# A block-sparse attention and channel-mixer kernel: another order of steps and other PSUM banks in its hand-written list

## The chip, the core and the metric

The kernel runs on one core of one Trainium2 chip. The engines named below are PE (TensorE, the matrix engine, with its weight loads shown apart as PEld), DVE (VectorE), ACT (ScalarE), POOL (GpSimd) and SP (SyncE, which here only issues DMAs). Each takes its own queue of instructions in order, and semaphores hold an instruction until what it reads is there and what it overwrites has been read. The metric is the device time of one execution in microseconds (us), as the median of several runs.

## The reference

Two layers, one behind the other: an attention under a block mask, and a mixer with a low-rank part along the sequence and a two-layer network along the channels.

```python
B, H, S, D = 4, 8, 768, 64
scores = q @ k.transpose(0, 1, 3, 2) / sqrt(D)
scores = where(mask, scores, -1e9)        # 32x32 blocks: neighbours, first and last, 3 drawn ones a row
attn = exp(scores - max) ; attn = attn / (sum(attn) + 1e-9)
x = (attn @ v).transpose(0, 2, 1, 3).reshape(B, S, 512)

h = x.transpose(0, 2, 1) @ U @ V          # U 768x32, V 32x768
u = x + h.transpose(0, 2, 1)
out = u + maximum(u @ w_ch1, 0) @ w_ch2   # w_ch1 512x2048, w_ch2 2048x512
```

Inputs and output are float32; the output is 4 x 768 x 512.

## The kernel before

The whole program is unrolled in one function. The 32 heads are taken as 16 pairs i = 0 to 15, four (HP) to a batch; a pair's queries and keys lie side by side in 128 partitions. For a pair the scores come out transposed (keys in partitions), so that exp(scores) can serve as the stationary operand of the product with v, whose extra column of ones gives the sums; masked entries are multiplied by 0 after exp. Per batch, the four pairs' results stand in `xf` (float32, one buffer of 128 x 6 x 512 a batch; the pool has two buffers, so batch 2 takes that of batch 0, and batch 3 that of batch 1) and in `xh` (float16). Then come the low-rank mix over the sequence, a transpose by DMA into `uT`, w1 with ReLU into `hid`, w2 into `xf`, and the stores. The w2 products are done in Winograd's form of Strassen's scheme (seven half-size products and sums of operands), as are the w1 products of the last batch. The attention of the next batch runs between the channel products of the one before.

PE, DVE, ACT and SP run in program order (`manual_schedule`, line 1112), and the program order is the string `PLAN` (lines 436 to 517): a loop (lines 1120 to 1131) takes it word by word. A word of capitals and a digit takes the next step of its kind and gives it the PSUM bank of that digit; a word in lower case runs the follow-up, on DVE or ACT, of an earlier product word of its kind, in the order in which these were queued; a word with dots calls a function with the numbers given. POOL is outside this order.

| word | what it issues | line |
|---|---|---|
| S, B, Q, H (plain) | scores of a pair into PSUM; Q (8 matmuls) does two heads in banks 0 to 5 | 951, 970, 1001 |
| e, p | exp on ACT; multiply by the mask on DVE | 960, 1010; 1016 |
| K, k | a part of the mask made on PE, its copy | 1085 on |
| A, V | products with v (V: all 36 matmuls of one head, into the bank of its digit) | 402 |
| v, y | divide on DVE (a reciprocal, then a product that reads the bank and writes `xf`); copy to `xh` on ACT | 532, 539; 537 |
| M, m, F, x, d | low-rank mix: Ut product, its copy on DVE, Vt product of two halves, add to `xf` on DVE, cast to `xh` on ACT | 638, 643, 653, 618, 622 |
| T.i | DMA transpose of pair i's `xh` into `uT`, on SP | 611 |
| U.b.c.j.bank, P, C | w1 product of batch b (4 matmuls of 384 columns) | 673 |
| a.b.c.j.e | its ReLU, e = 0 on DVE, 1 on ACT | 687, 685 |
| S.b.t.k, H.b.t.p.part, D.b.t.k | w2 in Winograd's form: sums of `hid` on DVE, half a product (4 matmuls of 256), add to `xf` on DVE | 843, 748, 867 |
| Z.b.t.u | store of row 2t+u of batch b (256 KB), on SP | 695 |
| L.i | loads(i+1): transposes of the casted q and k of pair i+2 (`qpl`, `kpl`), then loads of q, k and v of pair i+3 (384 KB each), on SP | 375, 150, 161 |
| q.k.n | a sum of weights for Winograd's form, on DVE | 709 |
| t, g, c, o, r, s | last batch: sums of inputs, w1 products, copies, sums, ReLUs, sums of `hid` | 709, 748, 782, 789 |
| h.t.p.part, e.t.k | last batch: quarter of a w2 product (2 matmuls of 256), its add on DVE; e also issues the store of half a row (128 KB) on SP | 748; 891, 893 |

A bank may be written anew only when the follow-up that reads it is done: so the digits decide, with the order, what a PE word waits for. Two more waits matter for the change. The first divide of pair 8 writes batch 2's `xf` and needs the stores `Z.0.*` to have landed, that of pair 12 writes batch 3's and needs `Z.1.*`. And an instruction of SP that waits (a transpose for its casts, or for the last product that reads the old `qpl`) holds every DMA behind it.

The loop that reads the list:

```python
for word in PLAN.split():
    kind = word[0]
    if "." in word:
        fn, *args = word.split(".")
        calls[fn](*map(int, args))
    elif kind.isupper():
        fn, *args = next(steps[kind])
        fn(*args, *map(int, word[1:]))
    elif kind in "ab":
        results["relu"].popleft()(kind)
    else:
        results[kind].popleft()()
```

Of the kernel before, what the change touches and what calls it, by code (L numbers as in the profile page):

```python
# [23 lines left out]
def kernel(  # L24
# [417 lines left out]
    y p H U7 e p H b C e p H b U7 e p H b U6 e p E1 a g p V7 Q v e e V6 U7 v p U0 a P1 b C p P6 a C E7 Q
    a g U6 e e U7 b P6 b p U0 C a U7 p a Q b X6 Y e e P7 y C P6 b C p U0 b a p V7 L.5 Q v U.0.1.3.6 e
    q.3.0 V7 a.0.1.3.0 e U.0.1.1.1 v U.0.1.11.0 a.0.1.1.1 U.0.1.5.6 q.3.1 a.0.1.11.1 p Q a.0.1.5.1 p
    U.0.1.10.6 e U.0.1.7.7 a.0.1.10.0 e U.0.1.2.6 a.0.1.7.0 S.0.0.1.3 U.0.1.9.7 p a.0.1.2.1 Q a.0.1.9.1
    q.7.1 U.0.1.4.6 e S.0.0.2.0 H.0.0.1.0.7 p H.0.0.1.1 a.0.1.4.1 U.0.1.0.0 p L.6 e U.0.1.14.1 q.4.1 V6
    a.0.1.0.1 p a.0.1.14.1 Q v q.4.0 e V6 D.0.0.0 S.0.0.3 H.0.0.6.0 e v U.0.1.13.2 q.7.0 H.0.0.6.1
    U.0.1.12.6 a.0.1.13.1 D.0.0.2 y p Q a.0.1.12.1 q.5.1 H.0.0.7.0 e H.0.0.7.1 q.5.0 H.0.0.5.0.6 D.0.0.3
    H.0.0.5.1 e S.0.0.4.4 U.0.1.6.1 p H.0.0.4.0 a.0.1.6.1 H.0.0.4.1 D.0.0.4 Q D.0.0.5 p H.0.0.3.0 e L.7
    H.0.0.3.1 p H.0.0.2.0.7 H.0.0.2.1 e p U.0.1.8.2 U.0.1.15.0 D.0.0.1 D.0.0.6 a.0.1.8.1 V7 p a.0.1.15.1  # L450
    S.0.1.1.1 Q S.0.2.1.0 V6 e v S.0.1.2.4 H.0.1.1.0.7 y v H.0.1.1.1 y H.0.1.2.0.0 S.0.2.2.3 y H.0.1.2.1
    e D.0.1.0 M6 D.0.1.1 H.0.2.1.0.1 m H.0.2.1.1 S.0.2.3 F.1.0.2.4 D.0.2.0 F.1.1.3.6 F.1.2.5.0 x.6.0
    H.0.2.6.0 x.6.1 d.6.0 H.0.2.6.1 x.7.0 d.6.1 F.1.3.6.4 D.0.2.2 H.0.1.6.0 T.6 x.5.1 H.0.1.6.1 S.0.1.3
    H.0.2.7.0 H.0.2.7.1 x.4.0 H.0.2.5.0.6 x.5.0 H.0.2.2.0.0 D.0.2.3 d.5.0 H.0.2.2.1 x.4.1 d.5.1
    H.0.2.4.0 D.0.1.2 d.4.0 T.5 x.7.1 H.0.2.4.1 d.7.0 H.0.1.7.0 D.0.2.1 d.4.1 D.0.2.5 H.0.1.7.1 d.7.1
    S.0.2.4.2 T.4 Q D.0.1.3 H.0.2.5.1 e H.0.1.4.0 T.7 D.0.2.4 H.0.1.4.1 H.0.2.3.0 e D.0.1.5 H.0.2.3.1
    Z.0.0.1 p H.0.1.5.0.7 Z.0.2.1 H.0.1.5.1 D.0.2.6 Q Z.0.2.0 D.0.1.4 Z.0.0.0 S.0.1.4.0 U.1.0.0.6 e
    H.0.1.3.0 a.1.0.0.0 H.0.1.3.1 e U.1.0.11.6 D.0.1.6 p U.1.0.10.0 Z.0.1.0 Z.0.1.1 a.1.0.11.1 U.1.0.9.7
    p L.8 a.1.0.10.1 U.1.0.6.6 a.1.0.9.1 p Q a.1.0.6.1 p U.1.0.12.6 e V7 e U.1.0.2.2 v U.1.0.5.0 p
    a.1.0.12.1 U.1.0.1.7 a.1.0.5.1 a.1.0.2.1 U.1.0.3.6 a.1.0.1.0 p Q a.1.0.3.1 V6 p e U.1.0.4.7 v e  # L460
    U.1.1.5.2 a.1.0.4.0 U.1.0.15.6 p a.1.1.5.1 U.1.1.9.7 a.1.0.15.1 p Q a.1.1.9.1 U.1.1.3.7 e L.9
# [701 lines left out]
```

## Time and profile before

| quantity | value |
|---|---|
| time of the runs | 274.29, 274.45, 274.58 us; median 274.45 |
| span of the profiled execution | 271.1 us, 7373 instructions |
| DMA | 37.58 MB, mean 139 GB/s |
| HBM read / written | 27.67 / 6.29 MB |
| exp of the Q words (line 1010) | 72 of 1450 ns, 100.6 us on ACT |
| w1 products (line 673) | 384 matmuls of 326 ns from start to end, 70.2 us |
| mask multiply (line 1016) | 72 of 933 ns, 65.5 us on DVE |
| divide's product (line 539) | 32 of 553 ns, 17.7 us on DVE |
| half-row stores (line 893) | 12 of 128 KB, 1.7 us from issue to landing |

The time of a run is that of the whole execution on the device; the span is that of the profiled execution, from its first to its last instruction; 3.35 us lie between the span and the median. Matmuls overlap: a matmul of 384 columns lasts 326 ns from start to end, and four of them follow each other in 0.65 us. What a word costs PE is this pitch, and the ends of its rows overlap with the next one's start. An instruction that reads a matmul's result begins some 0.2 us behind its end. Rows of the timelines begin with the start in us from the start of the span and the length; "x4" is a number of instructions in one row, and square brackets give the idle time before the row and what ended it.

### The profile page before, as it was taken

The page shows a single profiled execution, that of the slowest core. Times are in us where ns is not written, and L with a number is a line of the kernel's source. Part 1 is how long each engine was busy: PE and PEld are TensorE (multiplying, and loading weights), DVE is VectorE, ACT ScalarE, POOL GpSimd, SP SyncE. Part 2 cuts the span into 40 slices and gives each one's busy share as a digit, 9 for nine tenths or more (in the row PEclk, how much of TensorE's full clock was granted, in tenths as well). Part 3 has the DMA queues.
Part 4 walks back from the last instruction along what each step waited for, and adds up shares of the span by engine and source line. Part 5 has one row for each costly group of instructions (what it writes and reads, how often), then busy time and mean ns, then how long its engine had stood idle before and what let it go on. Part 6 is the DMA issues. An engine that isn't in the chain of part 4 may idle for free.

```text
span 271.1 us, 7373 instructions
## 1 busy us (share of the span) xinstructions
PE 261.9 (97%) x3008; PEld 182.1 (67%) x3008; DVE 235.3 (87%) x475; ACT 202.5 (75%) x264; POOL 84.7 (31%) x164
## 2 busy tenths in 40 slices
PE   7899999999999999999999999999999999999993
PEld 3577776555567778565666877565667788657882
DVE  5699988988999998868688997688998999999992
ACT  3889998897989666788888847788997943889100
POOL 4479104931628643035624660044000000000000
PEclk9999999999999999999999999999999999999998
DMA  5799997999974664872527356670200116300024
GB/s 161 239 305 316 199 210 173 225 131 198 155 222 67 201 204 91 278 217 59 178 45 190 64 212 117 221 208 16 46 0 2 41 41 142 134 0 0 22 78 136
DMA packets 49698, 37.58 MB, mean 139 GB/s; under 512 B 30528, under 2 KB 46816, under 8 KB 49664
## 3 DMA queue, kind: packets, MB, share of 16 engines
q1 hardware_dynamic: 46688, 32.67, 45.9%
q0 software_dynamic: 2688, 4.19, 10.9%
q8 instruction: 23, 0.38, 0.6%
q10 hardware_dynamic: 288, 0.24, 0.3%
q14 instruction: 11, 0.09, 0.1%
HBM read 27.67 MB, written 6.29 MB: 125 GB/s over the span
## 4 chain that ended last, share of the span: by engine, by line
PE 72%; DVE 17%; DMA 4%; ACT 2%; issue 1%; SPq 1%; POOL 0%; DVEq 0%; ACTq 0%
PE ps L748 28%; PE ps L673 20%; PE ps L402 9%; PE ps L1001 8%; DVE est L1016 5%; DMA qld<-in_q_dram 3%; PE ps L951 2%; DVE xf L867 2%; DVE xf L539 2%; DVE sums L843 1%; DVE res L709 1%; DMA vld<-in_v_dram 1%; ACT est L1010 1%; PE ps L970 1%; DVE sums L709 1%
## 5 line engine op out<-in xcount | busy, mean ns | idle before, releaser
L1010 ACT ACTIVATE est<-ps 128x1536 f16<-128x1536 f32 x72 | 100.6, 1450 | 18.9 <-PE ps L1001 18.9
L673 PE MATMUL ps<-uT,w1t 128*128 128x384 f16 x384 | 70.2, 326 | 0.2 <-DVE hid L687 0.2
L1016 DVE TENSOR_TENSOR est<-est,mask 128x1440 f16<-128x1440 f16 x72 | 65.5, 933 | 0.2
L673 PEld LDWEIGHTS <-w1t 128*128 128x128 f16 x384 | 35.6, 98 | 26.9 <-issue 7.0
L402 PEld LDWEIGHTS <-est 128*128 128x128 f16 x1152 | 40.2, 97 | 7.2 <-ACT hid L685 1.3
L402 PE MATMUL ps<-vt,est 128*128 128x65 f16 x1152 | 43.3, 193 | 0.1
L142 POOL CAST stqld<-qld 128x192 f16<-128x192 f32 x40 | 19.9, 540 | 73.2 <-DMA qld<-in_q_dram 36.0
L748 PEld LDWEIGHTS <-hid 128*128 128x128 f16 x360 | 34.3, 98 | 7.0 <-issue 1.9
L685 ACT ACTIVATE hid<-ps 128x384 f16<-128x384 f32 x63 | 29.7, 495 | 4.7 <-PE ps L673 4.3
L1001 PE MATMUL ps<-qpl,kpl 64*128 64x512 f16 (+1 forms) x288 | 31.6, 325 | 0.0
L748 PE MATMUL ps<-w2t,hid 128*128 128x256 f16 x240 | 31.3, 273 | 0.2 <-DVE xf L539 0.2
L867 DVE TENSOR_TENSOR xf<-xf,ps 128x256 f32<-128x256 f32 x63 | 25.0, 411 | 3.7 <-PE ps L748 3.3
L687 DVE TENSOR_SCALAR hid<-ps 128x384 f16<-128x384 f32 x33 | 18.2, 553 | 8.1 <-PE ps L673 7.5
L748 PEld LDWEIGHTS <-sums 128*128 128x128 f16 x216 | 20.3, 98 | 4.7 <-issue 1.1
L142 POOL CAST stkld<-kld 128x192 f16<-128x192 f32 x40 | 22.3, 597 | 2.5 <-DMA kld<-in_k_dram 2.5
L960 ACT ACTIVATE est<-ps 128x768 f16<-128x768 f32 x30 | 22.5, 813 | 0.6 <-PE ps L951 0.6
L1001 PEld LDWEIGHTS <-kpl 64*128 64x128 f16 x288 | 12.1, 94 | 14.3 <-issue 9.1
L748 PE MATMUL ps<-res,sums 128*128 128x256 f16 x144 | 19.4, 273 | 0.3 <-DVE xf L867 0.3
L622 ACT CAST xh<-xf 128x384 f16<-128x384 f32 x24 | 11.0, 510 | 10.4 <-DVE xf L618 10.4
L539 DVE TENSOR_TENSOR xf<-ps,rcp 128x384 f32<-128x384 f32 x32 | 17.7, 553 | 0.8
L142 POOL CAST vt<-vld 128x192 f16<-128x192 f32 x40 | 17.9, 487 | 0.0
L748 PE MATMUL ps<-res,hid 128*128 128x256 f16 x120 | 15.9, 273 | 0.0
(121 smaller groups left out, 341.5 us busy)
## 6 DMA issues: line engine op xcount, KB each, us to landing
vld<-in_v_dram SPq DMA_DIRECT2D x16, 384.0 KB, 4.6
qld<-in_q_dram SPq DMA_DIRECT2D x15, 384.0 KB, 3.5
kld<-in_k_dram SPq DMA_DIRECT2D x15, 384.0 KB, 5.5
out_dram<-xf SPq DMA_DIRECT2D x18, 256.0 KB, 2.2
w1t<-in_moe_w_ch_dram POOLq DMA_DIRECT2D x4, 512.0 KB, 8.2
w2t<-in_moe_w_ch_dram POOLq DMA_DIRECT2D x4, 512.0 KB, 10.4
out_dram<-xf SPq DMA_DIRECT2D x12, 128.0 KB, 1.7
qld<-in_q_dram SPq DMA_DIRECT2D x2, 192.0 KB
```

The costliest lines, as they stand in the source:

```text
L142: last = nc.gpsimd.tensor_copy(out=dst[:, h, ts], in_=ld[:, h, ts])
L402: nc.tensor.matmul(pav[:, sc, :], est[:, n, sc * P : (sc + 1) * P], vts[b % 2][:, 2 * hp + h, g, 0 : D + 1], start=(g == 0 and sc == 0), s ...
L539: nc.vector.tensor_tensor(out=dst, in0=pav[:, :, 0:D], in1=rcp[:, :, None].broadcast_to([P, T, D]), op=ALU.mult,)
L673: nc.tensor.matmul(pt, w1t[:, cc, jj * P : (jj + 1) * P], bts[b].uT[:, cc, c * HS : (c + 1) * HS], start=(cc == 0), stop=(cc == NCC - 1), ...
L685: nc.scalar.activation(out=dst, in_=pt, func=AF.Relu)
L687: nc.vector.tensor_scalar_max(out=dst, in0=pt, scalar1=0.0)
L748: nc.tensor.matmul(acc[key], lhsT, rhs, start=(first and i == 0), stop=(i == len(pairs_) - 1), skip_group_check=True,)
L867: nc.vector.tensor_add(out=x, in0=x, in1=acc[a, b, tau])
L960: lambda: nc.scalar.activation(out=dst, in_=ps, func=AF.Exp, scale=0.125),
L1001: nc.tensor.matmul(units[h][:, u * S + lo : u * S + hi], kT[drows[h], g * P : (g + 1) * P], qT[drows[h], lo:hi], start=True, stop=True, sk ...
L1010: nc.scalar.activation(out=both[h], in_=units[h].rearrange("p (g n) -> p g n", g=2), func=AF.Exp, scale=0.125,)
L1016: lambda: nc.vector.tensor_mul(out=masked(both[h]), in0=masked(both[h]), in1=masked(mask[:, 2 * j : 2 * j + 2, :]),),
```

## The change

The diff replaces the string `PLAN`; nothing else in the file differs. The new string is three lines shorter, so that what stands behind it moves up by three lines. It has the same words in another order: as many of each kind, dotted words with the same numbers but for the banks, the same split of ReLUs between DVE and ACT. 130 of the 574 product words name another bank. Most words move a few places. Of SP's DMAs, the stores change their place most: in batch 1 the old list has `Z.1.1.1 T.10 T.8 T.11 T.9 Z.1.1.0 Z.1.0.1 Z.1.2.0 Z.1.0.0 Z.1.2.1 L.12`, the new one `Z.1.1.1 Z.1.0.0 T.8 Z.1.0.1 T.10 T.11 T.9 Z.1.2.0 L.12 Z.1.1.0 Z.1.2.1`. The two products with v of pair 12 (`V6` and `V7` in the old list, with `v` behind each) are both `V7` in the new one. The start, the end of batch 1 with the beginning of pair 12, and the tail:

```diff
--- before.py
+++ after.py
@@ -434,86 +434,83 @@
 
 
     PLAN = """
-    S0 S3 e e S5 B0 e Z7 e S3 z Z6 e z B0 A7 A e R6 S3 t A R5 e A B0 t A K6 e A S3 k v A5 A e K6 k B0 A
-    A e K7 A K6 k S3 k A K7 e v B0 k S3 e M6 e A5 A m R7 A t B0 K6 R3 e k A A t S6 A e v S0 D2 S3 e d A7
-    A e A S0 K6 A e S3 k K2 A e S5 k A e v S3 R2 e S5 t S0 e M7 e S3 m D2 e B5 d A0 D1 e A A d A S3 D2 A
...
-    H.1.0.3.0 D.1.1.4 M4 S.1.2.2.0 H.1.0.3.1 m D.1.1.5 F.2.0.5.4 F.2.1.0.1 D.1.0.6 Z.1.1.1 H.1.2.1.0.6
-    x.8.0 H.1.2.1.1 x.10.0 d.8.0 H.1.1.3.0 x.10.1 d.10.0 F.2.2.7.5 D.1.2.0 F.2.3.4.2 d.10.1 H.1.2.2.0.1
-    x.8.1 T.10 H.1.2.2.1 x.11.0 H.1.1.3.1 x.9.0 d.11.0 H.1.2.6.0 x.11.1 d.8.1 H.1.2.6.1 d.9.0 D.1.1.6
-    T.8 H.1.1.2.0.7 D.1.2.1 d.11.1 x.9.1 H.1.1.2.1 S.1.2.3 d.9.1 Q T.11 D.1.2.2 D.1.1.1 e H.1.2.7.0
-    H.1.2.7.1 T.9 H.1.2.5.0.7 D.1.2.3 e H.1.2.5.1 S.1.2.4.2 H.1.2.4.0 Z.1.1.0 H.1.2.4.1 Z.1.0.1 Q
-    D.1.2.5 D.1.2.4 U.2.0.4.6 p e H.1.2.3.0 a.2.0.4.0 H.1.2.3.1 e U.2.0.12.6 D.1.2.6 U.2.0.5.7 Z.1.2.0
-    Z.1.0.0 a.2.0.12.1 Q Z.1.2.1 a.2.0.5.0 p U.2.0.2.7 e L.12 U.2.1.8.6 a.2.0.2.0 U.2.1.1.7 a.2.1.8.1 e
-    U.2.0.11.2 a.2.1.1.0 U.2.0.15.6 p a.2.0.11.1 U.2.0.0.7 p Q a.2.0.0.1 p a.2.0.15.1 U.2.0.9.7 e V6
-    a.2.0.9.0 p e U.2.0.8.0 v U.2.0.10.7 a.2.0.8.1 U.2.1.4.6 a.2.0.10.0 p Q a.2.1.4.1 V7 p e U.2.1.0.6 v
-    e U.2.0.13.1 a.2.1.0.0 U.2.0.1.7 p a.2.0.13.1 U.2.1.2.6 a.2.0.1.1 p Q a.2.1.2.0 U.2.1.9.7 e L.13
...
-    h.0.3.0 e.1.3 h.0.3.1 h.0.3.2 e.1.4 h.0.3.3 e.0.5 h.2.3.0 h.1.4.0 e.0.6 h.1.4.1 h.1.3.0 h.1.3.1
-    h.1.3.2 h.1.3.3 h.2.4.1 h.2.4.2 h.2.4.3 h.1.4.2 h.1.4.3 e.2.5 h.2.3.1 e.1.6 h.2.3.2 h.2.3.3 e.1.5
-    e.2.6
+    S0 e Z7 z S3 S5 e e B1 e Z0 A7 A A S5 z B0 e e S3 e A R6 t R5 t B0 e K4 k K6 A A v A5 A A k S3 B0 e e K7
+    K3 K4 k k A A A v S6 e B0 M3 m k R7 A5 A A S3 e e B0 e t K7 K3 k k A R4 t S6 A A v S0 e e S2 e D7 d A6 A
+    A S0 S4 K2 k e e A A A v S0 S3 e e R2 t M7 m S5 e S0 S3 e e D2 B5 A0 D1 d d D2 d A A A e S3 A A K1 k S5
...
+    H.1.1.4.0 S.1.2.2.0 y y y M2 m D.1.1.5 Z.1.1.1 H.1.0.3.1 H.1.0.3.0 D.1.0.6 Z.1.0.0 F.2.0.5.0 x.8.0 d.8.0
+    F.2.1.3.2 x.8.1 d.8.1 x.10.1 T.8 x.10.0 d.10.0 d.10.1 Z.1.0.1 T.10 H.1.2.1.0.6 H.1.2.1.1 D.1.2.0
+    H.1.1.3.1 H.1.1.3.0 D.1.1.6 F.2.2.2.7 x.11.0 d.11.0 x.9.0 d.9.0 F.2.3.1.3 x.11.1 d.11.1 T.11 x.9.1 d.9.1
+    T.9 H.1.2.2.0.5 H.1.2.2.1 D.1.2.1 H.1.1.2.0.7 H.1.2.6.0 H.1.2.6.1 D.1.2.2 Q e e S.1.2.3 H.1.1.2.1
+    D.1.1.1 H.1.2.7.0 H.1.2.7.1 D.1.2.3 S.1.2.4.2 H.1.2.5.0.7 H.1.2.5.1 D.1.2.4 H.1.2.4.1 H.1.2.4.0 D.1.2.5
+    p Q e e U.2.0.4.6 a.2.0.4.0 H.1.2.3.0 H.1.2.3.1 D.1.2.6 Z.1.2.0 U.2.0.12.6 a.2.0.12.1 U.2.0.5.7
+    a.2.0.5.0 q.0.1 Q e L.12 Z.1.1.0 U.2.0.2.7 a.2.0.2.0 U.2.1.8.6 a.2.1.8.1 U.2.1.1.7 p a.2.1.1.0 p p p e
+    U.2.0.15.2 a.2.0.15.1 U.2.0.11.1 a.2.0.11.1 U.2.0.0.6 a.2.0.0.1 Q e e U.2.0.9.6 a.2.0.9.0 V7 U.2.1.4.1
+    a.2.1.4.1 U.2.0.8.6 a.2.0.8.1 Q e e p p Z.1.2.1 v U.2.0.10.6 a.2.0.10.0 V7 v y y U.2.1.0.6 a.2.1.0.0
+    U.2.0.13.2 a.2.0.13.1 U.2.0.1.7 a.2.0.1.1 Q e e p p q.0.0 U.2.1.2.7 a.2.1.2.0 U.2.0.7.6 a.2.0.7.0 q.1.1
+    U.2.1.9.7 a.2.1.9.0 p U.2.0.6.0 a.2.0.6.1 U.2.0.14.6 a.2.0.14.1 Q e e p V7 p V6 v y v p U.2.0.3.7
...
+    h.1.2.2 e.1.1 h.2.4.2 h.0.4.3 h.2.3.1 h.0.4.0 h.0.3.0 h.0.4.2 h.0.4.1 h.2.4.3 h.2.3.2 e.0.5 h.0.3.1
+    h.0.3.3 h.0.3.2 e.0.6 e.2.5 h.1.3.0 h.1.3.3 h.1.4.2 h.1.3.2 h.1.3.1 e.1.6 h.2.3.3 h.2.3.0 e.2.6 h.1.4.3
+    h.1.4.0 h.1.4.1 e.1.5
     """
 
     class Pair:
```

More of the change, by code (lines that the diff above doesn't have):

```diff
@@ L442 @@
[L442 to L461, printed above, removed]
@@ new lines @@
+    S.0.0.3 D.0.0.2 H.0.0.7.0 q.7.1 H.0.0.7.1 p p q.5.0 H.0.0.5.0.6 H.0.0.5.1 D.0.0.3 D.0.0.4 p e p
+    U.0.1.6.2 a.0.1.6.1 H.0.0.4.1 Q L.6 L.7 H.0.0.4.0 D.0.0.5 H.0.0.3.0 H.0.0.3.1 D.0.0.6 e p e p
+    H.0.0.2.0.7 H.0.0.2.1 D.0.0.1 U.0.1.8.2 a.0.1.8.1 U.0.1.15.6 a.0.1.15.1 S.0.2.1.0 S.0.1.1.1 S.0.2.2.3 Q
+    e e V7 v y V6 v y H.0.2.1.0.1 H.0.2.1.1 D.0.2.0 S.0.1.2.4 H.0.1.1.0.7 H.0.1.1.1 D.0.1.0 M0 m H.0.1.2.0.3
+    H.0.1.2.1 S.0.2.3 F.1.1.4.2 x.4.1 F.1.0.0.6 x.4.0 d.4.0 d.4.1 x.6.1 d.6.1 T.4 H.0.2.6.1 H.0.2.6.0
@@ new lines @@
+    D.0.2.2 H.0.1.6.1 x.6.0 d.6.0 T.6 F.1.2.5.4 F.1.3.2.0 x.7.1 x.5.1 x.7.0 x.5.0 d.5.0 d.5.1 d.7.0 T.5
+    Z.0.0.0 d.7.1 T.7 Z.0.0.1 H.0.2.7.0 H.0.1.6.0 H.0.2.7.1 D.0.2.3 D.0.1.2 S.0.1.3 H.0.2.5.0.6 H.0.2.2.0.2
+    H.0.2.2.1 D.0.2.1 D.0.1.1 H.0.2.4.1 H.0.2.4.0 D.0.2.5 S.0.2.4.2 H.0.1.7.0 H.0.1.7.1 D.0.1.3 Q e e
+    H.0.2.5.1 D.0.2.4 S.0.1.4.0 H.0.1.4.0 H.0.1.4.1 D.0.1.5 H.0.2.3.0 H.0.2.3.1 D.0.2.6 p H.0.1.5.0.7
+    H.0.1.5.1 D.0.1.4 Q e e U.1.0.0.6 a.1.0.0.0 H.0.1.3.0 H.0.1.3.1 D.0.1.6 Z.0.1.0 U.1.0.6.6 a.1.0.6.1
@@ new lines @@
+    U.1.0.9.1 a.1.0.9.1 U.1.0.11.2 a.1.0.11.1 U.1.0.10.6 a.1.0.10.1 Q e e p p p p p Z.0.2.1 Z.0.2.0 V7
+    Z.0.1.1 v y U.1.0.12.6 a.1.0.12.1 U.1.0.1.2 p a.1.0.1.0 U.1.0.2.0 a.1.0.2.1 U.1.0.5.4 a.1.0.5.1
+    U.1.0.3.7 a.1.0.3.1 Q e V7 v U.1.0.4.6 a.1.0.4.0 p e U.1.0.15.1 a.1.0.15.1 y U.1.1.5.7 a.1.1.5.1
+    U.1.1.9.6 a.1.1.9.1 Q e e U.1.0.7.6 p a.1.0.7.0 U.1.1.3.7 a.1.1.3.0 p p U.1.0.14.6 a.1.0.14.1 U.1.1.4.2
+    a.1.1.4.0 U.1.1.10.1 a.1.1.10.1 U.1.1.1.6 a.1.1.1.1 L.8 Q e e V7 p V6 v U.1.1.7.7 a.1.1.7.1 y Q e e v
@@ new lines @@
+    c.5.1.2 c.3.1.3 c.2.1.1 c.1.1.0 g.0.1.2 c.0.1.9 D.2.2.4 H.2.2.3.1 H.2.2.3.0 Z.2.0.0 t.1 t.2 q.6.1
+    D.2.2.6 g.2.6 g.1.2.7 o.1.1 g.5.2.1 o.5.1 t.4 t.3 c.2.2.4 g.1.6 c.1.2.2 g.5.6 c.5.2.0 g.0.6 g.3.6
+    c.3.2.5 c.0.2.10 g.3.2.4 o.3.1 g.0.2.7 g.1.7 c.1.3.7 g.2.7 o.0.1 c.2.3.9 q.2.1 q.2.0 g.3.7 g.1.5.4 o.1.3
+    r.1.0.0 g.3.5.7 c.3.3.3 o.3.3 r.3.0.0 g.2.4 o.2.4 g.3.4 o.3.4 g.1.4 o.1.4 g.0.7 g.1.3 o.1.2 r.1.1.1
+    g.4.1.6 c.4.1.11 c.0.3.3 g.3.3 o.3.2 r.3.1.0 g.2.5.0 o.2.3 g.5.7 c.5.3.6 g.5.5.4 s.3.1.22 s.3.3 g.6.1.1
```

84 lines of the change are left out of this document (40 added, 44 removed).

## The prediction

> **What bounds the kernel now.** I read the busy times first, then the chain of waits, then the stretches, and last the timelines of the places that the new list touches.
>
> ```profile
> PE 261.9 (97%) x3008; PEld 182.1 (67%) x3008; DVE 235.3 (87%) x475; ACT 202.5 (75%) x264; POOL 84.7 (31%) x164
> PE 72%; DVE 17%; DMA 4%; ACT 2%; issue 1%; SPq 1%; POOL 0%; DVEq 0%; ACTq 0%
> ...
> 0.00:43.00 43.00, 39.39 (x518) 27.72 (x518) 34.65 (x79) 36.83 (x44) 20.55 (x36) 1.00 0.92 238
> 70.00:100.00 30.00, 29.30 (x374) 20.24 (x372) 29.72 (x52) 23.84 (x30) 18.83 (x32) 1.00 0.62 153
> 100.00:224.00 124.00, 123.52 (x1482) 85.51 (x1479) 106.16 (x194) 98.43 (x125) 33.60 (x72) 1.00 0.43 115
> 224.00:267.00 43.00, 42.90 (x342) 32.79 (x336) 39.98 (x108) 21.01 (x46) 0.00 (x0) 1.00 0.23 68
> 267.00:271.00 4.00, 0.00 (x0) 0.00 (x0) 0.36 (x1) 0.00 (x0) 0.00 (x0) 0.84 0.40 133
> ```
>
> The first line is busy time by engine, the second the chain that ended last, the others are stretches (length, then busy us of PE, weight loads, DVE, ACT and POOL, granted clock, DMA share, GB/s). TensorE works in 97% of the span and is 72% of the chain; from 100 to 267 us it lacks 0.6 us of 167. It is short of work only in the first 43 us (3.6 us), between 70 and 100 us (0.7 us, while VectorE is busy 29.72 of 30) and in the last 4 us, which are the final add and its store. The clock is 1.00 until the matmuls end. So a new order gains only in these holes, and loses wherever it lets something come after TensorE needs it.
>
> **What the change does not touch.** Both lists have 1277 words, each kind as often as before: 574 words that issue 3008 matmuls, the same 475 VectorE and 264 ScalarE instructions, 128 DMAs on SP, also the same split of ReLUs between ScalarE and VectorE. TensorE's work is therefore the same to the instruction; GpSimd's queue keeps its order. What is added and removed costs nothing; what moves is priced below, against the 271.1 us of this span. The remaining 3.35 us of the 274.45 median lie around it and stay.
>
> **Part 1: two stores go behind the loads (+1.2).** Pair 12's first divide writes xf of batch 3, whose buffer was batch 1's (two buffers), so it waits until every store of batch 1 has landed. The old list issues all six before L.12; the new one issues Z.1.1.0 after L.12 and Z.1.2.1 later still, both in SP's queue behind two front transposes and three 384 KB loads. SP, loads, VectorE and TensorE there:
>
> ```profile
> 172.43 1.31 SPq L695 DMA_DIRECT2D out_dram<-xf  x3
> 174.12 1.25 SPq L375 DMA_TRANSPOSE qpl<-stqld  x1
> 175.47 1.23 SPq L375 DMA_TRANSPOSE kpl<-stkld  x1
> 176.75 0.58 SPq L150 DMA_DIRECT2D qld<-in_q_dram  x1
> 177.38 0.46 SPq L150 DMA_DIRECT2D kld<-in_k_dram  x1
> 177.88 0.47 SPq L161 DMA_DIRECT2D vld<-in_v_dram  x1
> ...
> 178.00:180.00 2.00, 2.00 (x30) 1.18 (x29) 1.55 (x3) 1.78 (x3) 0.00 (x0) 1.00 0.96 296
> 180.00:182.00 2.00, 2.00 (x36) 1.48 (x32) 1.77 (x4) 2.00 (x3) 1.69 (x4) 1.00 0.81 283
> 182.00:184.00 2.00, 2.00 (x32) 1.11 (x31) 1.87 (x3) 1.06 (x3) 2.00 (x5) 1.00 0.06 19
> ...
> 181.03 0.19 DVE L532 RECIPROCAL rcp<-ps 128x6 f32<-128x6 f32 x1
> 181.25 0.56 DVE L539 TENSOR_TENSOR xf<-ps,rcp 128x384 f32<-128x384 f32 x1
> ...
> 183.43 1.26 PE L402 MATMUL ps<-vt,est 128*128 128x65 f16 x36
> ...
> out_dram<-xf SPq DMA_DIRECT2D x18, 256.0 KB, 2.2
> ```
>
> SP issues one DMA in about 0.45 us here, so the two stores leave at about 178.4 and 178.85, right behind the load of v. The three loads (3 x 393 KB = 1.18 MB) move in 178 to 182: 2 us at 296 GB/s and 2 us at 283 are 1.16 MB, after which the DMA engines idle (0.06). If the stores' packets stand behind the loads' packets, their 2 x 262 KB = 0.524 MB take 1.7 us (at 315 GB/s, the highest slice of the page's first part) to 1.85 us (at 283) from 182 on: landed at about 184.0. The divide (reciprocal to end 0.78) then runs its product from 184.0 to 184.6. The new list puts both value products of pair 12 into bank 7 (before: 6 and 7), so the second one, which stands at 183.43, cannot begin before that divide has read the bank: 184.6 + 0.05 - 183.43 = **1.2 us** of TensorE's time. Waiting with the divide on VectorE are the second head's divide, the mask multiplies of the quads behind it and the ReLUs on VectorE, all of whose readers on TensorE stand behind the second value product and so move with it (the mask multiplies, 0.90 each, serve value products some 4 us later); I count nothing more.
> Bounds: if stores pass the loads, they land 178.85 + 2.2 = 181.05 and nothing waits (0). If each store takes its whole 2.2 us one after the other, after the last load has landed at 177.88 + 4.6 = 182.5, they end at 186.9 and TensorE waits 186.9 + 0.6 + 0.05 - 183.43 = 4.1 us. I take 1.2: the DMA share 0.96 and 0.81 says that the loads fill the engines, the nearest row to what the stores meet.
> [...] The trace's whole store takes 2.2 us, about 0.9 of it data at these rates, so at most 1.3 us is fixed; the sum above has none of it, since the first store's fixed part runs beside the loads.
>
> **Part 2: what the low-rank mix waits for (-0.4).** In batch 2 the old list runs M4, one H word, the copy m (queued behind a pair sum), then F:
>
> ```profile
> 159.07 0.52 PE L638 MATMUL ps<-xh,Ut 128*32 128x128 f16 x24
> 159.17 0.79 DVE L709 TENSOR_TENSOR sums<-sums,hid 128x1024 f16<-128x1024 f16 x1
> ...
> 159.88 0.41 DVE L643 CAST a<-ps 128x256 f16<-128x256 f32 x1
> ...
> 160.34 0.51 PE L653 MATMUL ps<-a,Vt 64*128 64x128 f16 x12 [0.21 <-DVE a L643]
> ```
>
> The H word between (4 matmuls, 0.44 by pitch) ends at 159.95 and F begins 160.34: a hole of 0.39. The new list has M2 with both H words behind it and the pair sum ahead of it. The copy can then start 0.2 after M2's end; M (0.44 by pitch), two H words (0.88) against copy 0.20 + 0.41 + 0.05 = 0.66: F waits for nothing, or 0.1 if the copy stands behind a divide. I take 0.3 of 0.39. In batch 3 the old list has the copy late by 0.24 behind one H word (product at 220.21); with two it is hidden, I take 0.1. Bounds: 0 to -0.63.
>
> **Part 3: the tail (-0.3).** Old: the last two row stores are issued back to back and the very last waits for SP; new: three words h (h.1.4.3, h.1.4.0, h.1.4.1) stand between e.2.6 and e.1.5, which now ends alone.
>
> ```profile
> 265.85 1.51 DVE L891 TENSOR_TENSOR xf<-xf,ps 128x256 f32<-128x256 f32 x4 [1.69 <-PE ps L748]
> 256.00 12.09 SPq L893 DMA_DIRECT2D out_dram<-xf  x12
> ```
>
> The last add ends at 267.36; its store is issued 267.69 to 268.09, because SP was with the one before until 267.60. The three words (2 matmuls each, 0.22 by pitch) put the earlier store 0.66 before the last, longer than SP's 0.40 for it: the 0.33 of waiting goes. Bounds: 0 to -0.33.
>
> **Part 4: the other local moves (+0.2).** From the rows: ScalarE and VectorE start 0.2 us after the end of what they read, TensorE 0.05 after theirs. Walking both new queues along TensorE's old times, product by product, the new order is late at few places after 100 us: a ReLU that stands behind a weight sum by 0.07, a value product that waits for its mask multiply at about 217.6 by 0.12. I take 0.15 of these. In the first 43 us exp and mask copies are late by 0.1 to 0.6 at six places (largest a mask step behind an exp near 14 us), but the old order has waits there too (3.6 us of hole), which the new one meets differently; I take +0.1, bounds -0.6 and +0.6. From 70 to 100 us VectorE is full in both and does the same work: 0, bounds -0.6 (TensorE's hole) and +1.0 (rival C). The transposes T keep their place against their readers (first product that needs one stands 0.2 us behind its landing at about 228.8); stores of batch 2 go later, and nobody waits for that buffer.
>
> **Sum:** 1.2 - 0.4 - 0.3 + 0.15 + 0.1 = about +0.75; 274.45 + 0.75 = **275.2 us**. Its own range: the stall between 0.6 and 2.2 with the rest fixed gives 274.6 to 276.2; 0.6 is half of the stores' bytes getting out beside the loads, 2.2 adds 1.0 of the 1.3 us that a store's 2.2 leave beside its data.
>
> **Rivals.**
> *B, the stores are not held (chance 0.27).* The packets of the stores go out beside those of the loads that were issued before them. For it: vld lands 4.6 us after issue, so three loads were in flight at once in the trace; against it: the engines were at 0.96. Then Part 1 is 0 and the sum -0.45: 274.0. This is the case on the other side; it decides where the stores land before 182.8, so that the divide frees bank 7 by 183.43. Half of it falls under -0.55, half is no change. [...]
> *C, VectorE loses its fill at 70 to 100 us (0.15).* Its slack is 0.28 us there. The same multiplies (0.90), sums (0.68 to 0.79) and divides stand in another order, and one product that waits for a multiply placed behind one more sum of 0.7 costs TensorE this much, not caught up while VectorE is full. On top of A that is 275.2 + 0.8 = 276.0.
> *D, the new order fills the holes (0.08).* Half of the 3.6 + 0.7 us that TensorE lacks before 100 us comes back, about 2 us, with Part 1 small: about 272.5. Against it: the start waits for exp and loads (ScalarE 36.83 of 43, DMA 0.92), whose amount is the same.
> *That the list is only shuffled without effect* is part of "same": 3008 matmuls in the same clock.
>
> **Chances and range.** A 0.50, B 0.27, C 0.15, D 0.08. About 0.2% (0.55 us) is what a measurement can tell from no change: the bounds are 273.9 and 275.0. Faster: D 0.08, half of B 0.13, A's lower end 0.02: 0.23. Same: the other half of B, and of A what falls under 275.0 (0.08): 0.22. Slower: 0.40 of A and C: 0.55. The range reaches from B's lower part, 273.2, to 277.2, where C ends with the long stall (274.45 - 0.45 + 2.2 + 1.0).
>
> **What would show it.** Right: the divide of pair 12's first head starts some 1.2 us after the value products that feed it could let it, after an idle stretch of VectorE ended by a DMA (the store of row 5, Z.1.2.1), and TensorE idles about 1.2 us before the second value product of 36 matmuls; SP's timeline has two stores behind the load of v. F of batch 2 without a wait; the last store issued within 0.1 us of its add. Wrong: no hole near 183 us (B); TensorE busy less than 28.6 of the 30 us from 70 to 100 (C); more than 41 of the first 43 (D).

## The result, and the profile after

The new list is slower. Against the old one on the same chip the ratio of the times is 1.0102, with an interval of 1.0058 to 1.0147 (6 executions each: median 277.7 us against 274.5). Measured again in the last group of experiments, with 12 executions, the ratio was 1.0048 (1.0017 to 1.0079; 276.7 against 274.9). Both intervals hold 1.006 to 1.008, some 1.6 to 2.2 us. (A ratio is not the quotient of the two medians beside it, and executions more than 1.5% above the fastest of their kernel are left out of it, one of the 12 here.) The forecast was slower, 275.2 us in a range of 273.2 to 277.2: the direction held, but the first median lies above the range, and the loss is more than twice the forecast 0.75 us.

One thing must be known to read these times. Executions of either list begin in one of two ways: in some, TensorE's first matmuls run at full speed (327 ns for 384 columns) from 5.6 us on, in others (527 ns at first) only from 9.7 to 12.9 us on, which leaves them 1.7 to 2.6 us further behind at 62 us (four traces). The profiled executions of the old and the new list (spans 271.1 and 273.6 us) both have the early start, so that they can be compared line by line. About 1.8 us lie around a span (275.34 us for 273.56), not the 3.35 us that the prediction took.

The page of the new kernel, engine sums and the chain that ended last:

```profile
PE 263.8 (96%) x3008; PEld 180.9 (66%) x3008; DVE 235.7 (86%) x475; ACT 202.2 (74%) x264; POOL 82.8 (30%) x164
...
PE 59%; DVE 15%; DMA 11%; POOL 7%; SPq 3%; ACT 2%; issue 2%; POOLq 0%; DVEq 0%
```

Stretches of the same trace (length, busy us of PE, PEld, DVE, ACT and POOL, granted clock, DMA share, GB/s):

```profile
0.00:43.00 43.00, 39.98 (x502) 27.11 (x503) 34.26 (x79) 36.62 (x44) 20.11 (x35) 1.00 0.89 236
70.00:100.00 30.00, 29.28 (x360) 19.50 (x360) 28.71 (x49) 24.50 (x30) 19.91 (x37) 1.00 0.57 160
178.00:190.00 12.00, 10.37 (x129) 6.24 (x129) 8.17 (x14) 9.87 (x14) 4.77 (x12) 1.00 0.52 160
224.00:267.00 43.00, 43.00 (x355) 32.37 (x353) 41.27 (x110) 21.99 (x49) 0.00 (x0) 1.00 0.23 68
```

The hole is where it was expected: from 178 to 190 us TensorE lacks 1.63 us, where in the old list it was busy all 12. The stretch from 70 to 100 us is as full as before (29.28 against 29.30). TensorE's share of the last chain falls from 72% to 59%, and DMA, at 4% before, has 11%. That does not mean that DMAs cost 11%: the chain can run through any wait, and TensorE is busy for 96% of the span where it was for 97%.

To say where the difference arises, I took from each trace the start of every word's first matmul and subtracted the pitches of all words before it. What is left is TensorE's loss up to there; the list with the larger loss is behind.

| TensorE's loss, us, at | old list | new list | added difference |
|---|---|---|---|
| 41 us | 13.70 | 14.30 | 0.60 |
| 62 us | 16.50 | 17.16 | 0.06 |
| 105 us | 19.12 | 20.31 | 0.53 |
| 178 us | 22.11 | 23.61 | 0.31 |
| 200 us | 23.04 | 26.09 | 1.55 |
| 225 us | 23.86 | 26.82 | -0.09 |
| last words | 23.89 | 26.94 | 0.09 |
| last matmul to the end | 4.24 | 3.62 | -0.62 |

The column adds up to the 2.4 us between the spans (271.14 and 273.56). Around 183 us the new kernel's SP queue, VectorE and TensorE read:

```profile
178.22 0.58 SPq L150 DMA_DIRECT2D qld<-in_q_dram  x1
178.85 0.46 SPq L150 DMA_DIRECT2D kld<-in_k_dram  x1
179.36 0.47 SPq L161 DMA_DIRECT2D vld<-in_v_dram  x1
179.87 0.94 SPq L692 DMA_DIRECT2D out_dram<-xf  x2
...
183.50 0.18 DVE L529 RECIPROCAL rcp<-ps 128x6 f32<-128x6 f32 x1
186.13 0.56 DVE L536 TENSOR_TENSOR xf<-ps,rcp 128x384 f32<-128x384 f32 x1 [2.45 <-issue]
...
184.29 0.82 PE L670 MATMUL ps<-uT,w1t 128*128 128x384 f16 x4
186.75 1.27 PE L402 MATMUL ps<-vt,est 128*128 128x65 f16 x36 [1.63 <-POOL vt L142]
```

The two stores leave SP behind the load of v. The reciprocal of pair 12's first head is done at 183.68, its product with `xf` begins 2.45 us later, and the second value product, due at 184.95 by pitch, begins at 186.75, right after that product (end 186.69): 1.8 us lost. The brackets are no help here. "issue" means that no wait could be put down at all, and the matmul's wait is charged to a cast on GpSimd that ended at about the same time (186.7 us). Which of the two it was is the first question of the experiments. The data of loads and stores, by stretches of the same trace:

```profile
181.00:183.00 2.00, 2.00 (x44) 1.63 (x42) 1.76 (x3) 2.00 (x2) 1.07 (x2) 1.00 1.00 326
183.00:185.00 2.00, 2.00 (x16) 0.81 (x14) 0.69 (x2) 1.74 (x4) 2.00 (x6) 1.00 0.89 339
185.00:185.45 0.45, 0.11 (x1) 0.00 (x0) 0.00 (x0) 0.45 (x1) 0.45 (x2) 1.00 0.10 41
185.45:186.13 0.68, 0.00 (x0) 0.00 (x0) 0.00 (x0) 0.68 (x2) 0.68 (x4) 1.00 0.00 0
```

Nearly all bytes are through by about 185.0 us, and the divide starts 1.1 us after that. In the first 0.45 us of these a few of the 16 DMA engines still move data (the last packet ends at 185.44); then nothing moves for 0.7 us.

### The profile page after: what moved, and what is told of

The parts are those of the page before. It is cut to its first block, busy times and chain, and to the rows that moved or that the text cites. A ratio compares the mean times of both kernels' runs of the same rounds, so it can differ in the third digit from the quotient of the medians.

```text
span 273.6 us, 7361 instructions
## 1 busy us (share of the span) xinstructions
PE 263.8 (96%) x3008; PEld 180.9 (66%) x3008; DVE 235.7 (86%) x475; ACT 202.2 (74%) x264; POOL 82.8 (30%) x164
## 4 chain that ended last, share of the span: by engine, by line
PE 59%; DVE 15%; DMA 11%; POOL 7%; SPq 3%; ACT 2%; issue 2%; POOLq 0%; DVEq 0%
PE ps L745 29%; PE ps L670 12%; PE ps L402 7%; DMA vld<-in_v_dram 6%; PE ps L998 6%; DVE est L1013 5%; DMA kld<-in_k_dram 5%; POOL stkld L142 2%; SPq L375 2%; DVE xf L536 2%; POOL stqld L142 1%; DVE xf L864 1%; ACT est L957 1%; PE ps L948 1%; DVE sums L706 1%
## 5 line engine op out<-in xcount | busy, mean ns | idle before, releaser
L402 PEld LDWEIGHTS <-est 128*128 128x128 f16 x1152 | 39.2, 97 | 8.7 <-DVE xf L536 2.3
L402 PE MATMUL ps<-vt,est 128*128 128x65 f16 x1152 | 41.9, 193 | 2.3 <-POOL vt L142 1.6
L142 POOL CAST stqld<-qld 128x192 f16<-128x192 f32 x40 | 18.2, 496 | 73.4 <-issue 42.4
L998 PE MATMUL ps<-qpl,kpl 64*128 64x512 f16 (+1 forms) x288 | 31.5, 325 | 0.0
L142 POOL CAST stkld<-kld 128x192 f16<-128x192 f32 x40 | 20.7, 557 | 1.3 <-DMA kld<-in_k_dram 1.2
L142 POOL CAST vt<-vld 128x192 f16<-128x192 f32 x40 | 19.3, 522 | 3.1 <-DMA vld<-in_v_dram 3.1
```

Of the source, the lines that this page charges most:

```text
L142: last = nc.gpsimd.tensor_copy(out=dst[:, h, ts], in_=ld[:, h, ts])
L402: nc.tensor.matmul(pav[:, sc, :], est[:, n, sc * P : (sc + 1) * P], vts[b % 2][:, 2 * hp + h, g, 0 : D + 1], start=(g == 0 and sc == 0), s ...
L998: nc.tensor.matmul(units[h][:, u * S + lo : u * S + hi], kT[drows[h], g * P : (g + 1) * P], qT[drows[h], lo:hi], start=True, stop=True, sk ...
```

## The experiments

Each kernel is one of the two lists with a few words moved, or one list up to a word and the other from there on. Moving a store needs no other edit.

**The stores ahead of the loads, in the new list**

```diff
-    a.2.0.5.0 q.0.1 Q e L.12 Z.1.1.0 U.2.0.2.7
+    a.2.0.5.0 q.0.1 Q e Z.1.1.0 Z.1.2.1 L.12 U.2.0.2.7
...
-    Q e e p p Z.1.2.1 v U.2.0.10.6
+    Q e e p p v U.2.0.10.6
```

> The new list with the two stores Z.1.1.0 and Z.1.2.1 put ahead of L.12 in SP's queue, all else as in the new list. Theory (stores held behind three loads): the idle time of VectorE before the divide of pair 12's first head (2.45 us) and TensorE's jump of 1.81 us ahead of its second value product both go; TensorE is 1.5 us behind the old list before that point and stays there; span about 271.7 us (273.6 - 1.9), ratio to before about 1.002 to 1.004. Rival (the second value product waits for GpSimd's cast of v, which ended 0.04 us ahead of it): the jump stays at 1.5 us or more and the span at 273.3 or above. Of the spread between executions (275.3 and 277.7 us in the runs of the new list): if it comes from how late the stores land, the runs of this kernel agree within 1 us; if it comes from elsewhere, it stays.

The ratio is 1.0035 (0.9999 to 1.0070). The profiled execution has the late start (span 273.9 us), so the site is read by itself; VectorE, then TensorE:

```profile
185.59 0.18 DVE L529 RECIPROCAL rcp<-ps 128x6 f32<-128x6 f32 x1
185.81 0.56 DVE L536 TENSOR_TENSOR xf<-ps,rcp 128x384 f32<-128x384 f32 x1
...
186.37 0.83 PE L670 MATMUL ps<-uT,w1t 128*128 128x384 f16 x4
187.03 1.26 PE L402 MATMUL ps<-vt,est 128*128 128x65 f16 x36
```

The divide follows its reciprocal at once, and the value product follows the w1 product in its pitch of 0.66 us. The wait is gone though the loads and GpSimd's casts are still there: the store was the cause, and the bracket with GpSimd names a bystander. The expected span was missed, because of the late start; so was the guess that the spread between executions comes from the stores, since the times still run from 273.0 to 277.4 us.

**The same two stores behind the loads, in the old list**

```diff
-    H.1.2.4.0 Z.1.1.0 H.1.2.4.1 Z.1.0.1 Q
+    H.1.2.4.0 H.1.2.4.1 Z.1.0.1 Q
...
-    Z.1.0.0 a.2.0.12.1 Q Z.1.2.1 a.2.0.5.0 p U.2.0.2.7 e L.12 U.2.1.8.6
+    Z.1.0.0 a.2.0.12.1 Q a.2.0.5.0 p U.2.0.2.7 e L.12 Z.1.1.0 Z.1.2.1 U.2.1.8.6
```

> The old list with only the two stores Z.1.1.0 and Z.1.2.1 moved behind L.12. Theory: they land near 184.6 us (186.1 in the new list, whose TensorE ran 1.5 us later), the divide of pair 12's first head ends near 185.2, and the w1 product that takes bank 6 after it (at about 182.0 in the old list) waits about 3.2 us: more than in the new list, whose digits put this wait 1.4 us later; span about 273.5 to 274.5, ratio about 1.010 to 1.012. Rival (the order of stores alone is harmless, the new banks and GpSimd's cast make the wait): no jump over 0.5 us near 182 us, ratio within 1.003.

The ratio is 1.0183 (1.0135 to 1.0232), more than expected. Timelines of VectorE and TensorE:

```profile
185.31 0.56 DVE L536 TENSOR_TENSOR xf<-ps,rcp 128x384 f32<-128x384 f32 x1 [3.53 <-DMA out_dram<-xf]
...
185.92 1.44 PE L670 MATMUL ps<-uT,w1t 128*128 128x384 f16 x4 [3.27 <-DVE xf L536]
187.29 1.46 PE L998 MATMUL ps<-qpl,kpl 64*128 64x512 f16 x8
```

Stretches of it, two in the wait and one behind it:

```profile
182.65:185.00 2.35, 0.01 (x1) 0.00 (x0) 0.00 (x0) 0.08 (x1) 2.28 (x9) 1.00 0.64 243
185.10:185.90 0.80, 0.00 (x0) 0.00 (x0) 0.59 (x2) 0.00 (x0) 0.10 (x1) 0.50 0.00 0
185.90:191.00 5.10, 5.08 (x50) 2.99 (x50) 2.18 (x4) 2.64 (x3) 0.00 (x0) 0.50 0.01 3
```

Here the trace names the releaser, the store. The w1 product that takes bank 6 waits 3.4 us, as expected (3.2). But the granted clock falls to 0.50 inside the wait, at 185.05 us, 2.4 us into a wait that the bracket gives as 3.27, and stays there until 191.9 us: a Q word takes 1.46 us in place of 0.82, and 2.8 us are lost on top; by 192 us the two stores have cost 6.2 us. So the order of the two stores alone makes the loss, and the new list's digits make it smaller: with bank 7 for both value products TensorE meets the wait one w1 product and a Q word later (1.4 us).

**One and three stores behind the loads, in the new list**

```diff
-    L.12 Z.1.1.0
+    Z.1.1.0 L.12
```

> The new list with Z.1.1.0 ahead of L.12 and only Z.1.2.1 behind it: one store behind the loads in place of two. Theory (the stores' bytes queue behind the loads' bytes): the divide starts 0.65 to 0.9 us earlier than with two, counted from the issue of the load of v, and TensorE's jump ahead of the second value product falls from 1.81 to about 1.0 us. Rival (the fixed end of a DMA, not bytes, sets the landing): the jump stays within 0.3 us of 1.81. Second rival (stores pass the loads): no jump.

```diff
-    D.1.2.6 Z.1.2.0 U.2.0.12.6
+    D.1.2.6 U.2.0.12.6
...
-    L.12 Z.1.1.0
+    L.12 Z.1.2.0 Z.1.1.0 Z.1.2.1
...
-    p p Z.1.2.1 v
+    p p v
```

> The new list with Z.1.2.0 too put behind L.12: three stores behind the loads. Theory (bytes): the divide starts 0.65 to 0.9 us later than with two, counted from the issue of the load of v; TensorE's jump 2.4 to 2.8 us. Rival (fixed end of a DMA): the jump stays within 0.3 us of 1.81.

VectorE and SP with one store behind (first two lines), and with three:

```profile
178.98 0.47 SPq L161 DMA_DIRECT2D vld<-in_v_dram  x1
184.97 0.56 DVE L536 TENSOR_TENSOR xf<-ps,rcp 128x384 f32<-128x384 f32 x1 [1.65 <-issue]
```

```profile
178.28 0.47 SPq L161 DMA_DIRECT2D vld<-in_v_dram  x1
185.65 0.56 DVE L535 TENSOR_TENSOR xf<-ps,rcp 128x384 f32<-128x384 f32 x1 [3.03 <-DMA out_dram<-xf]
```

| stores behind the loads | issue of the load of v to the divide, us | TensorE's wait, us | ratio (interval) |
|---|---|---|---|
| 0 | no wait | 0 | 1.0035 (0.9999 to 1.0070) |
| 1 | 5.99 | 1.02 | 1.0015 (0.9975 to 1.0055) |
| 2 | 6.77 | 1.81 | 1.0102 (1.0058 to 1.0147) |
| 3 | 7.37 | 2.39 | 1.0135 (1.0090 to 1.0179) |

Each store adds 0.78 and 0.60 us, the second a little less than the expected 0.65 to 0.9. The other traces scatter by as much as 0.5 us (one store in the old list 5.44; two stores 6.90, 6.96 and 6.99), so no rate can be read from it. But the order holds: the more stores stood behind the loads, the later the divide that waits for them began (5.99, 6.77 and 7.37 us after the issue of the load of v). A landing set by the fixed end of a DMA alone would have left the wait at 1.8, and stores that pass the loads would have had none: both rivals fall.

**One list up to 120 us, the other from there**

> The old list up to 120 us (525 words), then the new one. Theory: the 1.2 us that TensorE has lost by 120 us in the new list (0.6 before 44 us, 0.6 between 70 and 100 us) are not lost; the stall at the stores stays 1.8 us or grows to 2; span about 272.4, ratio 1.004 to 1.007. Rival (the loss before 120 us is absorbed later, because the later stages wait for loads): span unchanged at 273.4 or above.

> The new list up to 120 us, then the old one. Theory: TensorE is 1.2 us late at 120 us and stays so, no jump over 0.5 us near 182 us; span about 272.3, ratio 1.003 to 1.006, and the two halves (this and the run with the old list first) add up to the whole change. Rival (absorbed later): ratio within 1.002.

The old list first: 1.0063 (1.0025 to 1.0101), and TensorE's wait at the stores is 1.99 us. The new list first: 1.0018 (0.9984 to 1.0051), no wait at 182 us; its profiled execution lost 3 us at 72 to 76 us to a late load of w2, so that its single stages compare only up to 62 us, where its loss is the new list's (17.04). That second ratio is below the expected 1.003 to 1.006 and is the one that the rival gave (a loss before 120 us is won back later). The trace speaks against the rival: word for word it is 3.2 us later than the old kernel's at 105 us (mostly by the late load) and 3.3 us at 225 us, so that nothing is won back. The first 120 us are thus the smaller part, but with intervals of 0.3% each way their size has to come from the traces.

**The old list up to 62 or 120 us, then the new one with the stores first**

> The old list up to 62 us (271 words), then the new one with the two stores ahead of L.12. Theory: the new list's own loss sits ahead of 62 us (0.65 us on the mean of the profiled executions, ScalarE's exp a little late each time) and not between 70 and 100 us, where executions of either list differ by 0.6 us with what GpSimd's casts meet; so TensorE's loss at 62 us is that of the old list (16.1 to 16.7 us against 17.0 to 17.2 in the new, for the same kind of start), and times are as in the run with the old list up to 120 us, ratio 0.998 to 1.001. Rival (the new order costs TensorE 0.5 us between 70 and 100 us): loss between words 62 us and 105 us larger by 0.4 us or more than in the old list's executions, ratio 1.002 or more.

> The old list up to 120 us, then the new one with Z.1.1.0 and Z.1.2.1 ahead of L.12. Theory: without the wait at the stores and without the first 120 us, what is left of the new list is a gain: TensorE's loss from 120 to 265 us is 0.2 to 0.6 us smaller than in the old list and the end (last matmul to the end of the span) is 3.65 us as in the new list against 4.2 in the old; times below those of the kernel before by 0.6 to 1.1 us, ratio 0.996 to 0.998. Rival (the new list's later part only looks better because the wait had left slack): the tail alone, ratio 0.998 to 1.000, and no loss recovered between 190 and 200 us.

Ratios: 0.9971 (0.9935 to 1.0007) and 1.0001 (0.9973 to 1.0029), the first a little below and the second above what was expected, though both intervals overlap with that; spans of the profiled executions, both with the early start, 270.7 us each against 271.1. Losses at 62 us: 16.52 and 16.16, as in the old list. The rival for 70 to 100 us seemed to be borne out by the first of the two: from 65 to 105 us it loses 2.87 us, the old list 2.28 in its first trace. But other executions of the old list's words lose 2.66, 2.60, 2.86, 2.75 and 2.36 there, and executions of the new list's 2.81, 2.58, 1.85, 2.63 and 2.70. With all of them the means are 2.59 and 2.57 (left out is the one with the late load of w2). The 0.53 us in the table above is thus no more than the spread of executions (1.85 to 2.87 us); a few tenths from the order would not be seen in it. From 183 to 225 us the new order without its wait loses 1.30 us in three executions, the old order 1.66 in two: a gain of 0.36. So the later part's gain is not the tail alone, as the rival had it.

**The tail alone**

```diff
-    h.1.4.2 h.1.4.3 e.2.5 h.2.3.1 e.1.6 h.2.3.2 h.2.3.3 e.1.5 e.2.6
+    h.1.3.1 e.1.6 h.2.3.3 h.2.3.0 e.2.6 h.1.4.3 h.1.4.0 h.1.4.1 e.1.5
```

(the diff shows its end; the last 36 words of the old list take the new order)

> The old list with only its last 36 words in the new order. Theory: the last store is issued right behind its add, so from the end of the last matmul to the end of the span it is 3.65 to 3.75 us in place of 4.2; the words before it do not change; times 0.4 us below those of the kernel before, ratio 0.998 to 0.999, which the interval will hardly tell from 1. Rival (the landing of the last store depends on the bytes queued ahead of it, not on its issue): 4.1 us or more.

The ratio is 0.9965 (0.9931 to 0.9998), the only kernel here whose interval lies below 1. Its last matmul ends at 269.22 us of a span of 273.1: 3.88 us against 4.24, somewhat more than the expected 3.65 to 3.75. The last store is issued at 269.71, 0.03 us behind its add, where the old list waited 0.33 us for SP. That is the 0.3 us of the prediction; the rest of the measured ratio (1 us) is not shown to come from the tail, and the interval allows for its absence.

**One store behind the loads, in the old list**

```diff
-    a.2.0.12.1 Q Z.1.2.1 a.2.0.5.0 p U.2.0.2.7 e L.12
+    a.2.0.12.1 Q a.2.0.5.0 p U.2.0.2.7 e L.12 Z.1.2.1
```

> The old list with only Z.1.2.1 behind L.12. With two stores behind it, TensorE idled 3.3 us at 182.6 us, its matmuls of 384 columns then took 525 ns in place of 326 until 191.7 us, and the whole cost 6.2 us. Theory: one store less shortens the idle time by its bytes (0.6 to 0.8 us) to 2.5 to 2.8 us, and whether the clock drops then decides the cost: without a drop 2.5 to 2.8 us, ratio 1.009 to 1.011; with a drop 5 us or more. The waits of 2.4 us and less seen so far brought no drop, so the first is likelier. Rival (the further loss is not the clock but the queue that VectorE works off after its wait): a further loss in proportion, 2 us or more, at full clock.

The ratio is 1.0100 (1.0052 to 1.0149). TensorE's timeline, and the stretch behind the wait:

```profile
184.56 0.81 PE L670 MATMUL ps<-uT,w1t 128*128 128x384 f16 x4 [1.80 <-DVE xf L536]
```

```profile
185.50:191.00 5.50, 5.50 (x71) 3.34 (x68) 4.58 (x8) 4.21 (x6) 0.00 (x0) 1.00 0.01 3
```

The wait was 1.97 us, shorter than the 2.5 expected; behind it the clock stays at 1.00 and nothing more is lost, so the further loss with two stores was the clock and not VectorE's queue. This is the quickest of its six executions (275.9 us). The mean clock of two others is 0.991, where the old kernel's 29 executions beside it have 0.994 or more: in these the drop may have come after all, but no trace shows it.

**A longer warm-up, in the old kernel**

```diff
-        keep_warm(8)
+        keep_warm(11)
```

> The old kernel with 11 instead of 8 dummy matmuls ahead of the first real one (line 303), the list untouched. It asks where the spread between executions of one kernel comes from. Theory: in some executions (the profiled ones of the old and the new list) matmuls of 384 columns take 326 ns from 5.6 us on, in others 525 ns until some 12 us, which costs 2.0 to 2.7 us; 8 matmuls of 0.43 us end at 4.2 us and TensorE then idles to 5.1 us. With 11 they end at 5.5 us, the slow start gets rarer and the median falls to about 273.3, ratio about 0.996. Rival (the start depends on the execution alone, not on how long TensorE has worked): both kinds of start as often as before, ratio 0.999 to 1.002.

The ratio is 1.0017 (0.9992 to 1.0042): nothing gained. No trace of an ordinary execution of it is there, so how its matmuls started is not shown; of the times, 4 of 11 lie below 274.0 us, against 20 of 35 of the kernel before, and 11 of 29 and 9 of 29 in the other groups. How to get the early start each time stays open.

**The new kernel again**

> The new kernel unchanged, in the same call as these three, for its ratio on the same chip. Theory: wait at the stores 1.6 to 2.0 us and the first 62 us 0.65 us, the end 0.5 us shorter: about 1.9 us, ratio 1.006 to 1.009; in executions where the wait comes to 2.5 us or more the clock may drop and cost 2 us more. Rival (the 1.0102 measured first is right, something beyond these terms costs 0.9 us): ratio 1.010 or more.

Ratio 1.0048 (1.0017 to 1.0079), below the expected 1.006 to 1.009, the lower part of which is inside the interval, while the rival's 1.010 is not; TensorE's wait at the stores is 2.02 us, and the trace puts it down to the store (a wait of VectorE of 2.66 us).

## Why the prediction was right in kind and wrong in size

The terms, each for like starts:

| step | predicted, us | measured, us |
|---|---|---|
| Part 1, stores behind loads | +1.2 | +1.8, 2.0 and 2.0 in three executions |
| Part 2, low-rank mix | -0.4 | -0.15 in batch 2, -0.13 in batch 3 |
| Part 3, tail | -0.3 | -0.62 (alone: -0.36) |
| Part 4, after 100 us | +0.15 | about 0 from 105 to 178 us and -0.36 from 183 to 225, each with its share of Part 2 in it |
| Part 4, the start (to 62 us) | +0.1 | +0.64 |
| Part 4, 70 to 100 us | 0 | 0.0 |
| sum | +0.75 | about +1.6 |

*Part 1: right mechanism, one term too small.* Place, cause and order of events were as forecast, and so was the time when nearly all bytes are through: about 183.8 us by the working, 185.0 in the trace, whose TensorE is 1.5 us later at this point. The step that failed is "landed at about 184.0": the prediction let the bytes end at full rate and gave 0.2 us from there to the wait's end, and the trace shows 1.1, of which 0.45 is the last of the DMA engines finishing and 0.7 comes behind the last packet (0.4 to 0.7 in the seven traces with stores behind loads). It had noted that up to 1.3 of a store's 2.2 us is not data, and left this out of the sum because it would run beside the loads. For a further store that fits the series (0.78 and 0.60 us each), but not for the last one, behind which nothing is queued: its 0.7 us count.

*Part 4, the start: the step that failed outright.* The new list loses 0.64 us more by 62 us (means of five old starts, 16.52, and four new ones, 17.16, all early). The prediction had seen late arrivals of 0.1 to 0.6 us at six places and set them off against the old order's own waits to +0.1, its bound being 0.6. In this stretch ScalarE runs its 39 exps (37.5 us) nearly without a gap, so that an exp that comes late is not caught up. Rows of ScalarE, old list and then new:

```profile
15.57 0.80 ACT L960 ACTIVATE est<-ps 128x768 f16<-128x768 f32 x1
...
22.75 7.24 ACT L960 ACTIVATE est<-ps 128x768 f16<-128x768 f32 x10
...
31.19 5.17 ACT L960 ACTIVATE est<-ps 128x768 f16<-128x768 f32 x7
```

```profile
16.08 0.81 ACT L957 ACTIVATE est<-ps 128x768 f16<-128x768 f32 x1 [0.49 <-PE ps L948]
...
22.94 7.38 ACT L957 ACTIVATE est<-ps 128x768 f16<-128x768 f32 x10
...
31.53 5.47 ACT L957 ACTIVATE est<-ps 128x768 f16<-128x768 f32 x7
```

In the new list an exp waits 0.49 us for its scores at 16 us, and the rows from 23 and from 31.5 us are 0.14 and 0.30 us longer with the same exps. Compared exp by exp, the new list gains 0.2 to 0.3 us up to 14 us and is then set back at four places (16, 26, 32 and 34 us); from the first exps to the last it falls behind by 0.44 to 0.51 us in each of the four early executions. So the setting-off failed: the old order's own waits did not make up for these. Which of the moved words does it was not taken apart.

*Part 2.* In batch 2 the wait before F fell from 0.39 to 0.24 us and not to 0.1. Rows of the new list there:

```profile
160.79 0.79 DVE L706 TENSOR_TENSOR sums<-sums,hid 128x1024 f16<-128x1024 f16 x1
...
161.50 0.41 DVE L640 CAST a<-ps 128x256 f16<-128x256 f32 x1
...
161.97 0.51 PE L650 MATMUL ps<-a,Vt 64*128 64x128 f16 x12
```

The prediction let the copy start 0.2 us after M2's end by pitch, at about 161.0; the pair sum ahead of it still held VectorE, and it started at 161.50. In batch 3 the gain is the 0.1 us that was forecast; the rest of the 0.36 us between 183 and 225 us comes from other moves and was not taken apart.

*Part 3.* The 0.33 us of SP's queue is gone, as worked out. Another 0.3 us lies behind the issue of the last store, 3.13 us before the end of the span against 3.45. This was not foreseen; six of the nine traces with the new tail show it, the tail alone (3.39) does not, and its cause stays open.

*The base.* Adding to 274.45 assumed that the profiled execution was a typical one with 3.35 us around it. It was one with an early start: 271.1 + 1.8 = 272.9, the lower end of the old kernel's times. That does not touch the difference, but it does the median: of the first six executions of the new kernel three lie about 2.2 us and one 3.6 us above the other two, as with a late start, and that put 277.7 beyond the range, where the second set's 276.7 lies inside it. Of these six only one was traced, so that the late starts among them are not shown.

*The rivals.* B (stores not held) falls by the series of one, two and three stores; with the stores first the new list is at 1.0035, its interval reaching to 1. C (70 to 100 us) is not there on the mean of the traces. D (holes filled) is not there either: 39.98 us of the first 43.

No version clearly beats the old kernel by more than the tail: the old list with the new tail is at 0.9965, at the edge of its interval.

## What to carry to other kernels

Look through a reordered list for stores, not only for matmuls: a buffer that is used again makes a store a producer, and here one, two and three stores behind three loads of 384 KB cost TensorE 1.02, 1.81 and 2.39 us. My estimate of such a wait, from the new list's trace: the bytes of the loads and of the stores at the rate of the stretch (326 and 339 GB/s), and once, for the last store, the 1.1 us after the bulk of the bytes. And compare traces whose executions began alike: one pair of traces showed 0.5 us at 70 to 100 us that the others took back.

## What was not expected of the hardware

- A wait cost more than itself: in 3.27 us without a matmul the granted clock fell to 0.50, and 2.8 us more were lost until 191.9 us. Waits of TensorE of 1.0 to 2.4 us left it at 1.00 in the profiled executions. No safe length follows from this: behind the last matmul the clock fell after 2.8 us in the old kernel's trace, and in the new one's it was still 1.00 at the end of the span, 3.6 us behind.
- The two kinds of start show in the same clock. The clock record begins with the rise to 1.00: between 3.4 and 4.9 us in the nine traces with an early start (3.44 us in the old kernel's, 4.57 in the new one's), at 9.7, 9.8, 12.5 and 12.9 us in the four with a late one (the stretches above show the time before the first record as 1.00). Matmuls of 384 columns in the first 12 us, grouped, in the execution with stores first (late start):

```profile
L948 PE MATMUL ps<-res 128*128 128x384 f16 x6 | 2.3, 527 | 0.0
```

and in the old kernel's (early start):

```profile
L951 PE MATMUL ps<-res 128*128 128x384 f16 x8 | 1.8, 327 | 0.5 <-DVE res L281 0.5
```

  527 against 327 ns each. The old kernel's times cluster near 273.4 us and between 274.5 and 276.5, likely for this reason; only one execution of it was traced.
- VectorE's mask multiplies took longer beside GpSimd's casts. In the old kernel's trace, a mask multiply while GpSimd casts v and one while it is idle:

```profile
73.17 2.36 POOL L142 CAST vt<-vld 128x192 f16<-128x192 f32 x4
...
74.28 1.04 DVE L1016 TENSOR_TENSOR est<-est,mask 128x1440 f16<-128x1440 f16 x1
...
78.83 0.90 DVE L1016 TENSOR_TENSOR est<-est,mask 128x1440 f16<-128x1440 f16 x1
```

  1.04 against 0.90 us; over the whole trace the median of the 20 multiplies beside casts is 1.02 us, that of the 44 alone 0.90. When the casts run depends on when the loads land (in the old kernel's trace the casts of q waited 36.0 us in all for their loads), and that differs between executions: the casts of v that begin at 73.17 us here begin at 68.20 us in the trace of the old list with the two stores behind the loads, whose words up to there are the same. I take it for a likely source of the spread between 65 and 105 us, where VectorE has little slack (29.72 of 30 us busy from 70 to 100; 2.3 to 2.9 us of loss with the old order); that link was not tested by itself.
